# Reordering one stretch of a fused attention and MLP kernel: kv a little later, two transposes together, one weight chunk earlier, one output later

## The chip, the cores and the metric

The kernel runs on one core of one Trainium2 chip. The metric is the device time of one execution in microseconds (us). In the profile, PE is TensorE, PEld its weight loads, DVE is VectorE, ACT ScalarE, POOL GpSimd, SP SyncE.

## The reference, cut to what matters

```python
def _attn_ref(q, k, v, phi):          # batch 8, heads 8, seq 576, head_dim 64, phi has 32 memory slots
    a = softmax(phi, axis=slots)
    k_m = einsum('bhsm,bhsd->bhmd', a, k)        # pooled k
    v_m = einsum('bhsm,bhsd->bhmd', a, v)        # pooled v
    attn = softmax(scale * q @ k_m^T)
    return attn @ v_m

def _moe_ref(x, g_ln, w_ch1, w_ch2):  # x: 8 x 576 x 512
    xn = layernorm(x) * g_ln
    return x + relu(xn @ w_ch1) @ w_ch2          # 512 -> 2048 -> 512
```

(Shortened; in the original the softmaxes and the norm are written out.) The kernel folds the pooled v into the first MLP weight: it makes W1b = pooled v times w_ch1 for each batch and then h = relu(W1b applied to the attention), so that the attention's output is never multiplied by w_ch1 itself.

Of the kernel before, what the change touches and what calls it, by code (L numbers as in the profile page):

```python
# [16 lines left out]
def kernel(  # L17
# [38 lines left out]
    def big(shape, dtype, name):  # L56
        return psum.tile(shape, dtype, name=name, tag="big", bufs=3)

    def one(shape, dtype, name):
        return psum.tile(shape, dtype, name=name, tag="one", bufs=2)  # L60
# [35 lines left out]
    def load(b):  # L96
        loaded[b] = (phis[b] if b > 2 else load_phi(b, nc.gpsimd), load_kv(b), load_q(b))
# [137 lines left out]
    def a_kv(b):  # L235
        ps = big([P, 2, 512], FP32, "kv_ps")
        kv_mm(b, ps, slice(0, 2))
        if b < 2:
            kv_sum(b, ps)
            rs_out(b, ps)  # L240
        k_out(b, ps, True)
        v_out(b, ps[:, :, D:2 * D])

    def a_tr(b, k_part=True, v_part=True):
        s = st8[b]
        t_ps = big([P, 3, P], BF16, "kvT_ps")
        if k_part:
            kvT = att.tile([P, 3, P], BF16, name="kvT")
            s["kvT"] = kvT
            for g in range(2):  # L250
                nc.tensor.transpose(t_ps[:, g, :], s["k2"][:, g].rearrange("p a d -> p (a d)"), ident)
        kvT = s["kvT"]
        if v_part:
            nc.tensor.transpose(t_ps[:, 2, :], s["v2"].rearrange("p a d -> p (a d)"), ident)
        if k_part:
            nc.vector.tensor_copy(out=kvT[:, 0:2, :], in_=t_ps[:, 0:2, :])
        if v_part:
            nc.vector.tensor_tensor(out=kvT[:, 2, :].rearrange("p (j m) -> p j m", m=M),  # L258
                                    in0=t_ps[:, 2, :].rearrange("p (j m) -> p j m", m=M),
                                    in1=g_bf.unsqueeze(2).to_broadcast([P, 4, M]), op=ALU.mult)  # L260
            rsum = att.tile([P, 2], FP32, name="rsum")
            nc.vector.tensor_reduce(out=rsum, in_=s["v2"], axis=mybir.AxisListType.X, op=ALU.add)
            s["rsum"] = rsum
# [9 lines left out]
    def a_vb(b):  # L273
        s = st8[b]
        vb = att.tile([P, 2, 4, D], BF16, name="vb", bufs=3)
        for g in range(2):
            vsl = s["v2"][:, g, :].unsqueeze(1).to_broadcast([P, 4, D])
            nc.vector.tensor_tensor(out=vb[:, g], in0=vsl, in1=vmask, op=ALU.mult)
        s["vb"] = vb

    def a_qT(b, i):
        s = st8[b]
        if b > 1:

            if i == 0:
                s["qT"] = att.tile([P, 4, NP, P], BF16, name="qT")
                nc.sync.dma_start_transpose(out=s["qT"].rearrange("p j n x -> p (j n) x"),
                                            in_=s["q"].rearrange("p j n x -> p (j n x)"))
            return
        if i == 0:  # L290
            s["qT"] = att.tile([P, 4, NP, P], BF16, name="qT")
        q_ps = big([P, 2, 1024], BF16, "qT_ps")
        for u in range(2):
            for n in range(NP):
                nc.tensor.transpose(q_ps[:, u, P * n:P * (n + 1)], s["q"][:, 2 * i + u, n, :], ident)
        dst = s["qT"][:, 2 * i:2 * i + 2].rearrange("p a n x -> p a (n x)")
        if i == 0 or b == 1:
            nc.scalar.activation(out=dst, in_=q_ps[:, :, 0:NP * P], func=AF.Copy)
        else:
            nc.vector.tensor_copy(out=dst, in_=q_ps[:, :, 0:NP * P])  # L300

    def a_sc(b):
        s = st8[b]
        kvT, qT = s["kvT"], s["qT"]
        E_ = att.tile([P, 2, 2 * HP], BF16, name="E_sb", bufs=1)
        for g in range(2):
            sc = big([P, 2, 512], FP32, "sc_ps")
            for j in range(4):
                for r in range(2):
                    nc.tensor.matmul(  # L310
                        sc[32 * j:32 * (j + 1), r, 0:HP],
                        kvT[64 * r:64 * (r + 1), g, 32 * j:32 * (j + 1)],
                        qT[64 * r:64 * (r + 1), j, :, TS * g:TS * (g + 1)],
                        start=True, stop=True, tile_position=(64 * r, 32 * j))
            nc.scalar.activation(out=E_[:, g].rearrange("p (a x) -> p a x", a=2),  # L315
                                 in_=sc[:, :, 0:HP], func=AF.Exp, scale=s["rs"][:, g:g + 1])
        s["E"] = E_

    def a_den(b, finish=True):
        s = st8[b]  # L320
        Eh = att.tile([P, 2, S], BF16, name="Eh", bufs=3)
        rd = att.tile([P, 2, 2, HS], FP32, name="rden", bufs=1)
        for g in range(2):
            den = big([P, 2, 512], FP32, "den_ps")
            for half in range(2):
                o = HS * half
                nc.tensor.matmul(den[:, half, 0:HS], blk, s["E"][:, g, o:o + HS],  # L327
                                 start=True, stop=True)
            nc.scalar.activation(out=rd[:, g], in_=den[:, :, 0:HS], func=AF.Ln)  # L329
        s["Eh"], s["rd"] = Eh, rd  # L330
        if finish:
            a_den2(b)

    def a_den2(b):
        s = st8[b]
        Eh, rd = s["Eh"], s["rd"]
        for g in range(2):
            nc.scalar.activation(out=rd[:, g], in_=rd[:, g], func=AF.Exp, scale=-1.0)  # L338
            nc.vector.scalar_tensor_tensor(  # L339
                out=Eh[:, g, :], in0=s["E"][:, g, 0:S],  # L340
                scalar=s["rs"][:, g:g + 1], in1=rd[:, g].rearrange("p a x -> p (a x)"),
                op0=ALU.mult, op1=ALU.mult)

    def a_w1b(b, n):
        s = st8[b]
        if n == 0:
            s["w1b"] = att.tile([P, 2, F], BF16, name="w1b", bufs=1)
        ps = big([P, 2, 512], FP32, "w1b_ps")
        fs = slice(512 * n, 512 * (n + 1))
        for j in range(4):  # L350
            for g in range(2):
                r = 64 * g
                nc.tensor.matmul(  # L353
                    ps[32 * j:32 * (j + 1), g, :], s["kvT"][r:r + 64, 2, 32 * j:32 * (j + 1)],
                    w1r[r:r + 64, j, fs], start=True, stop=True, tile_position=(r, 32 * j))
        for g in range(2):
            nc.vector.scalar_tensor_tensor(  # L357
                out=s["w1b"][:, g, fs], in0=m_sb[:, fs], scalar=s["rsum"][:, g:g + 1],
                in1=ps[:, g, :], op0=ALU.mult, op1=ALU.add)
# [72 lines left out]
    def mm2(pr, t, j0, j1, ps=None, finish=True):  # L432
        rT = pair[pr]
        if j0 == 0:
            chs[(pr, t)] = one([P, C], FP32, "ch_ps") if ps is None else ps
        ch_ps = chs[(pr, t)]
        for j in range(j0, j1):
            nc.tensor.matmul(ch_ps, rT[:, j, P * t:P * (t + 1)], w2b[:, j, :],  # L438
                             start=(j == 0), stop=(j == JC - 1))
        if j1 == JC and finish:  # L440
            mm2_out(pr, t)
# [17 lines left out]
    def mm2_out(pr, t):  # L459
        ch_ps = chs[(pr, t)]  # L460
        x, rstd = xs[(pr, t)]
        nc.vector.scalar_tensor_tensor(out=x, in0=ch_ps, scalar=rstd, in1=x,  # L462
                                       op0=ALU.mult, op1=ALU.add)
        for u in range(2):
            lo = P * t + TS * u
            dst = out[2 * pr + lo // S].rearrange("(p c) x -> c p x", c=NS)
            nc.sync.dma_start(out=dst[CO[lo % S // TS]], in_=x[TS * u:TS * (u + 1), :])
# [61 lines left out]
    a_exp(1)  # L529
    mm2(0, 0, 4, 16)  # L530
    mm2(0, 1, 4, 16)
    mm2(0, 2, 0, 4)
    a_kv(1)
    mm2(0, 2, 4, 8)
    a_tr(1)
    a_qT(1, 0)
    a_w1b(1, 0)
    mm2(0, 2, 8, 12)
    a_qT(1, 1)
    a_w1b(1, 1)  # L540
    mm2(0, 2, 12, 16)
    a_sc(1)
    mm2(0, 3, 0, 4)
    a_den(1)
    a_w1b(1, 2)
    mm2(0, 3, 4, 8)
    a_w1b(1, 3)
    a_vb(1)
    mm2(0, 3, 8, 16)
    load(2)  # L550

    for b in range(1, B):
# [69 lines left out]
```

## The kernel before: the parts that the change touches

There are three PSUM buffers of two banks each, which nearly all intermediate results share, and two of one bank for the output sums (PSUM is the memory that the matmuls write into):

```python
def big(shape, dtype, name):
    return psum.tile(shape, dtype, name=name, tag="big", bufs=3)
def one(shape, dtype, name):
    return psum.tile(shape, dtype, name=name, tag="one", bufs=2)
```

The steps of one batch's attention, cut to what each engine does:

```python
def a_kv(b):      # PE: pooled k and v -> kv_ps; ACT, DVE: read them out
def a_tr(b):      # PE: transposes of pooled k and v -> kvT_ps; DVE: read out
def a_qT(b, i):   # PE: ten transposes of half i of q -> qT_ps; ACT: read out (batch 1)
def a_sc(b):      # PE: scores -> sc_ps (two halves g); ACT: E_sb = exp(scores)
def a_den(b, finish=True):   # PE: sums of E_sb -> den_ps; ACT: ln, then exp(-ln); DVE: Eh = E_sb / sum
    ...
    if finish:
        a_den2(b)
def a_w1b(b, n):  # PE: chunk n of four of W1b -> w1b_ps; DVE: two evictions into w1b
    ...
    for g in range(2):
        nc.vector.scalar_tensor_tensor(
            out=s["w1b"][:, g, fs], in0=m_sb[:, fs], scalar=s["rsum"][:, g:g + 1],
            in1=ps[:, g, :], op0=ALU.mult, op1=ALU.add)
def mm1(b, j0, j1):   # PE: 4 matmuls per j -> h_ps; ACT or DVE: Relu into rT
def mm2(pr, t, j0, j1, ps=None, finish=True):   # PE: j1-j0 matmuls of output tile t -> ch_ps
    ...
    if j1 == JC and finish:
        mm2_out(pr, t)    # DVE: x = x + rstd * ch_ps; SP: two stores
```

In the traces here each engine's instructions come in the order of the program. From batch 2 on, a batch's attention is threaded into the ch_ps matmuls of the pair before by a general loop. Batch 1's is threaded by hand into those of batch 0, and this is the list that the change reorders:

```python
mm2(0, 1, 4, 16)
mm2(0, 2, 0, 4)
a_kv(1)
mm2(0, 2, 4, 8)
a_tr(1)
a_qT(1, 0)
a_w1b(1, 0)
mm2(0, 2, 8, 12)
a_qT(1, 1)
a_w1b(1, 1)
mm2(0, 2, 12, 16)
a_sc(1)
mm2(0, 3, 0, 4)
a_den(1)
a_w1b(1, 2)
mm2(0, 3, 4, 8)
a_w1b(1, 3)
a_vb(1)
mm2(0, 3, 8, 16)
load(2)
...
mm1(1, 0, JC)
```

The softmax here doesn't subtract the row's maximum and nothing guards it: scores larger than these inputs give would overflow.

## Time and profile before

| what | value |
|---|---|
| time, median of 3 runs | 257.77 us (257.45 to 258.12) |
| span of the profiled execution | 256.2 us |
| PE busy | 241.3 us, 94% |
| kv_ps of batch 1 starts | 42.86 us |
| first h_ps of batch 1 starts | 54.79 us |
| the 64 h_ps of batch 1 end | 58.97 + 5.15 = 64.12 us |

A row of a timeline has start and duration in us, engine, line, operation, out<-in, shape and count; in brackets stands how long the engine was idle before it and what ended that. I use one more number throughout: **from kv_ps to the end of h_ps**, here 64.12 - 42.86 = 21.26 us. It is meant to leave out when v landed.

### The profile page before, as it was taken

Reading aid. Unit: us, or ns where it says so; the run is one execution under the profiler, and the core shown is the slowest. Engines: PE = TensorE matmul, PEld = TensorE weight load, DVE = VectorE, ACT = ScalarE, POOL = GpSimd, SP = SyncE. Lnnn points to the kernel's source line nnn. Section 1 sums busy time; section 2 is a strip of 40 time slices with the busy share of each in tenths; the row PEclk is TensorE's granted clock in tenths of the full one; section 3 lists DMA queues with packets and bytes.
Section 4 is the critical chain, followed back from the end, with each engine's and each line's share of the span. In section 5 each row is a group of like instructions: output and inputs, shape, how many; then the busy total and the mean of one; then the engine's idle time right before and its main releaser. Section 6 shows DMA issues by size and latency. Waiting matters only on the chain.

```text
span 256.2 us, 5777 instructions
## 1 busy us (share of the span) xinstructions
PE 241.3 (94%) x2421; PEld 131.6 (51%) x2453; DVE 154.8 (60%) x306; ACT 129.0 (50%) x219; POOL 51.9 (20%) x87
## 2 busy tenths in 40 slices
PE   7968998999989999999999999999999999999994
PEld 2534554447534574457544664457444764466453
DVE  3236772675495954695486746694577648683431
ACT  3155662666545483547544582558253762565210
POOL 8642330000720007100630009000800022000000
PEclk9999999999999999999999999999999999999999
DMA  7999999999399383997399492969398441130133
GB/s 152 186 206 206 207 254 231 267 185 129 111 166 194 84 162 96 183 199 142 97 177 193 93 214 38 210 159 157 107 197 179 103 84 44 45 73 9 44 82 82
DMA packets 41922, 36.82 MB, mean 144 GB/s; under 512 B 17444, under 2 KB 37160, under 8 KB 41896
## 3 DMA queue, kind: packets, MB, share of 16 engines
q0 software_dynamic: 17248, 19.53, 44.9%
q1 hardware_dynamic: 24488, 16.79, 28.6%
q8 instruction: 19, 0.31, 0.5%
q10 hardware_dynamic: 160, 0.13, 0.2%
q14 instruction: 7, 0.06, 0.1%
HBM read 41.42 MB, written 9.44 MB: 199 GB/s over the span
## 4 chain that ended last, share of the span: by engine, by line
PE 81%; DMA 6%; DVE 4%; ACT 3%; POOL 2%; issue 2%; POOLq 0%
PE ch_ps L438 44%; PE h_ps L374 24%; DMA w1r<-in_moe_w_ch_dram 6%; PE w1b_ps L353 3%; PE o_ps L404 2%; PE kv_ps L205 2%; DVE w1b L357 2%; PE last_ps L450 1%; PE den_ps L327 1%; POOL kv_bf L84 1%; PE sc_ps L310 1%; DVE bst L416 1%; ACT rT L380 1%; POOL q_bf L92 1%; DVE Eh L339 1%
## 5 line engine op out<-in xcount | busy, mean ns | idle before, releaser
L438 PE MATMUL ch_ps<-w2b,rT 128*128 128x512 bf16 x530 | 126.0, 380 | 2.1 <-issue 1.1
L438 PEld LDWEIGHTS <-rT 128*128 128x128 bf16 x560 | 51.1, 98 | 62.6 <-issue 7.4
L374 PE MATMUL h_ps<-Eh,w1b 128*128 128x288 bf16 x512 | 67.4, 285 | 1.2 <-ACT rT L380 0.7
L380 ACT ACTIVATE rT<-h_ps 128x576 bf16<-128x576 f32 x88 | 52.6, 649 | 22.7 <-PE h_ps L374 22.5
L374 PEld LDWEIGHTS <-w1b 128*128 128x128 bf16 x512 | 49.5, 97 | 18.6 <-issue 2.9
L357 DVE SCALAR_TENSOR_TENSOR w1b<-m_sb,rsum,w1b_ps 128x512 bf16<-128x512 f32 x64 | 43.7, 742 | 3.2 <-ACT m_sb L169 2.4
L382 DVE TENSOR_SCALAR rT<-h_ps 128x576 bf16<-128x576 f32 x40 | 30.3, 757 | 24.1 <-PE h_ps L374 24.1
L410 ACT ACTIVATE x_sb<-o_ps 128x1024 f32<-128x1024 f32 (+1 forms) x20 | 18.6, 937 | 37.8 <-PE o_ps L404 36.5
L462 DVE SCALAR_TENSOR_TENSOR x_sb<-ch_ps,rstd,x_sb 128x512 f32<-128x512 f32 x35 | 26.1, 746 | 15.0 <-PE ch_ps L438 14.3
L189 POOL TENSOR_TENSOR es<-e_sb 128x512 f32<-128x512 bf16 x6 | 6.9, 1152 | 139.1 <-ACT e_sb L182 139.1
L416 DVE BATCH_NORM_STATS2 bst<-x_sb 128x6 f32<-128x512 f32 x36 | 24.4, 678 | 8.1 <-ACT x_sb L410 8.1
L339 DVE SCALAR_TENSOR_TENSOR Eh<-E_sb,rs,rden 128x576 bf16<-128x576 bf16 x16 | 12.4, 816 | 15.9 <-ACT rden L338 15.9
L315 ACT ACTIVATE E_sb<-sc_ps,rs 128x640 bf16<-128x640 f32 x16 | 11.9, 790 | 12.1 <-PE sc_ps L310 12.1
L424 ACT ACTIVATE rstd<-mv,eps_sb 128x2 f32<-128x2 f32 (+1 forms) x20 | 5.9, 296 | 20.3 <-DVE mv L417 20.3
L353 PE MATMUL w1b_ps<-w1r,kvT 64*32 64x512 bf16 x256 | 10.8, 383 | 0.9 <-DVE kvT L258 0.4
L174 PE MATMUL w_ps<-fill 128*128 128x512 f32 x14 | 9.7, 815 | 1.6 <-DVE fill L119 1.6
L227 DVE CAST v<-kv_ps 128x128 bf16<-128x128 f32 x8 | 2.3, 292 | 14.6 <-ACT k L220 13.7
L329 ACT ACTIVATE rden<-den_ps 128x576 f32<-128x576 f32 x16 | 9.6, 644 | 2.1 <-PE den_ps L327 2.1
L182 ACT ACTIVATE e_sb<-phi_st 128x1152 bf16<-128x1152 f32 x8 | 9.2, 1152 | 2.6 <-DMA phi_st<-in_phi_dram 2.6
L338 ACT ACTIVATE rden<-rden 128x576 f32<-128x576 f32 x16 | 10.0, 680 | 0.0
L205 PEld LDWEIGHTS <-e_sb 64*32 64x32 bf16 x648 | 6.3, 90 | 6.3 <-ACT e_sb L182 3.0
L205 PE MATMUL kv_ps<-kv_bf,e_sb 64*32 64x128 bf16 (+1 forms) x648 | 7.5, 214 | 1.9 <-issue 0.8
(69 smaller groups left out, 143.6 us busy)
## 6 DMA issues: line engine op xcount, KB each, us to landing
out_dram<-x_sb SPq DMA_DIRECT2D x70, 128.0 KB, 2.4
kv_bf<-in_k_dram POOLq DMA_DIRECT2D x7, 576.0 KB, 6.4
kv_bf<-in_v_dram POOLq DMA_DIRECT2D x7, 576.0 KB, 9.6
phi_st<-in_phi_dram SPq DMA_DIRECT2D x6, 576.0 KB, 4.5
q_bf<-in_q_dram POOLq DMA_DIRECT2D x6, 576.0 KB, 11.9
w1r<-in_moe_w_ch_dram POOLq DMA_DIRECT2D x4, 512.0 KB, 14.3
w2b<-in_moe_w_ch_dram POOLq DMA_DIRECT2D x4, 512.0 KB, 18.7
q_bf<-in_q_dram POOLq DMA_DIRECT2D x4, 288.0 KB, 12.5
```

What stands on the lines that cost most here:

```text
L205: nc.tensor.matmul(ps[32 * j:32 * (j + 1), g, 0:D * (sl.stop - sl.start)], e[r:r + TS, c, j, :], kv[r:r + TS, j, sl, D * c:D * (c + 1)], s ...
L315: nc.scalar.activation(out=E_[:, g].rearrange("p (a x) -> p a x", a=2), in_=sc[:, :, 0:HP], func=AF.Exp, scale=s["rs"][:, g:g + 1])
L339: nc.vector.scalar_tensor_tensor(out=Eh[:, g, :], in0=s["E"][:, g, 0:S], scalar=s["rs"][:, g:g + 1], in1=rd[:, g].rearrange("p a x -> p (a ...
L353: nc.tensor.matmul(ps[32 * j:32 * (j + 1), g, :], s["kvT"][r:r + 64, 2, 32 * j:32 * (j + 1)], w1r[r:r + 64, j, fs], start=True, stop=True, ...
L357: nc.vector.scalar_tensor_tensor(out=s["w1b"][:, g, fs], in0=m_sb[:, fs], scalar=s["rsum"][:, g:g + 1], in1=ps[:, g, :], op0=ALU.mult, op1 ...
L374: nc.tensor.matmul(h_ps[:, half, 0:HS], s["w1b"][:, g, P * j:P * (j + 1)], s["Eh"][:, g, HS * half:HS * (half + 1)], start=(g == 0), stop= ...
L380: nc.scalar.activation(out=dst, in_=h_ps[:, :, 0:HS], func=AF.Relu)
L382: nc.vector.tensor_scalar(out=dst, in0=h_ps[:, :, 0:HS], scalar1=0.0, scalar2=None, op0=ALU.max)
L410: nc.scalar.activation(out=x[:, 0:n].rearrange("p i (u y) -> p i u y", u=2), in_=o_ps.rearrange("p u (i y) -> p i u y", i=2)[:, 0:n], func ...
L416: nc.vector.bn_stats(out=stt, in_=x[:, i, :])
L438: nc.tensor.matmul(ch_ps, rT[:, j, P * t:P * (t + 1)], w2b[:, j, :], start=(j == 0), stop=(j == JC - 1))
L462: nc.vector.scalar_tensor_tensor(out=x, in0=ch_ps, scalar=rstd, in1=x, op0=ALU.mult, op1=ALU.add)
```

## The change

Its intent is to fill PE's pauses in this stretch: kv is asked for later, when v has landed; the two q transposes stand together, so that ScalarE can read them out one behind the other; the third W1b chunk goes ahead of the denominators; the output of tile 3 goes behind the last W1b. No instruction is added or taken away.

```diff
     mm2(0, 1, 4, 16)
-    mm2(0, 2, 0, 4)
+    mm2(0, 2, 0, 8)
     a_kv(1)
-    mm2(0, 2, 4, 8)
+    mm2(0, 2, 8, 12)
     a_tr(1)
     a_qT(1, 0)
+    a_qT(1, 1)
     a_w1b(1, 0)
-    mm2(0, 2, 8, 12)
-    a_qT(1, 1)
+    mm2(0, 2, 12, 16)
     a_w1b(1, 1)
-    mm2(0, 2, 12, 16)
     a_sc(1)
     mm2(0, 3, 0, 4)
+    a_w1b(1, 2)
     a_den(1)
-    a_w1b(1, 2)
-    mm2(0, 3, 4, 8)
+    mm2(0, 3, 4, 12)
     a_w1b(1, 3)
+    mm2(0, 3, 12, 16, finish=False)
     a_vb(1)
-    mm2(0, 3, 8, 16)
+    mm2_out(0, 3)
     load(2)
```

## The prediction

> **What bounds the kernel now.** I read the page first, then the chain of work in order of time, then the timelines of the engines in the one stretch that the change touches.
>
> ```profile
> PE 241.3 (94%) x2421; PEld 131.6 (51%) x2453; DVE 154.8 (60%) x306; ACT 129.0 (50%) x219; POOL 51.9 (20%) x87
> ...
> PE 81%; DMA 6%; DVE 4%; ACT 3%; POOL 2%; issue 2%; POOLq 0%
> ```
>
> TensorE (PE) is busy 94% of the 256.2 us span and is 81% of the chain that ended last, so the kernel is as long as PE's work plus PE's pauses. The change removes and adds no instruction and reorders only the stretch in which batch 1's attention is threaded into the second matmul (ch_ps) of batch 0. Of all that can happen, only PE's pauses in that stretch count. The stretch is from the end of the ch_ps matmuls of tile 1 (42 us) to the end of batch 1's h_ps group (64.2 us). In the chain in order of time its parts that are not PE's work are:
>
> ```profile
> 42.06 0.80 issue
> 42.86 0.93 PE kv_ps L205 x72
> ...
> 49.54 1.48 ACT E_sb L315 x2
> 51.02 1.14 ACT rden L329 x2
> 52.16 0.58 ACT rden L338
> ...
> 52.76 1.55 DVE Eh L339 x2
> 54.31 1.33 DVE w1b L357 x2
> ```
>
> The reader should see a pause of 0.8 us ahead of kv_ps that the profile cannot name ("issue"), and then a chain through ScalarE and VectorE from the scores (sc_ps) to h_ps. The unnamed pause gets its name from where the transfers were issued and how long each took to land; the first block is GpSimd's timeline, the second the list of transfers (size, us from issue to landing) for each of these two issues alone:
>
> ```profile
> 23.25 0.74 POOL L84 DMA_DIRECT2D kv_bf<-in_v_dram  x1 [1.80 <-DMA w1r<-in_moe_w_ch_dram]
> ...
> 28.38 0.71 POOL L92 DMA_DIRECT2D q_bf<-in_q_dram  x1 [1.88 <-DMA w2b<-in_moe_w_ch_dram]
> ```
> ```profile
> kv_bf<-in_v_dram POOLq DMA_DIRECT2D x1, 576.0 KB, 19.5
> ...
> q_bf<-in_q_dram POOLq DMA_DIRECT2D x1, 288.0 KB, 18.3
> ```
>
> So batch 1's v lands at 23.25 + 19.5 = 42.75, and kv_ps starts at 42.86: the pause is a wait for v. The second half of q lands at 28.38 + 18.3 = 46.7 (the first, issued at 25.80 and 19.1 us under way, at 44.9). PE's own rows show when they are used, and two further pauses:
>
> ```profile
> 47.13 0.72 PE L295 MATMUL qT_ps<-ident,q_bf 128*128 128x128 bf16 x10
> ...
> 51.07 0.41 PE L327 MATMUL den_ps<-E_sb,blk 128*128 128x288 bf16 x2 [0.22 <-ACT E_sb L315]
> ...
> 55.69 1.15 PE L374 MATMUL h_ps<-Eh,w1b 128*128 128x288 bf16 x8 [0.24 <-DVE w1b L357]
> 57.09 1.63 PE L374 MATMUL h_ps<-Eh,w1b 128*128 128x288 bf16 x12 [0.25 <-ACT rT L380]
> ```
>
> The first q transpose runs at 45.17, the second at 47.13, only 0.4 us after its data landed. The h_ps group pauses three times (55.69, 57.09 and 58.97). A printed pause runs from the modelled end of the last matmul, so I count from starts instead: the 64 h_ps matmuls of batch 2 take 7.96 us in the chain (124 ns each), batch 1's take from 54.79 to 64.17, 9.38, so 1.2 to 1.4 us is lost there. By starts the pause at kv_ps is 0.9 us, at den_ps 0.4, at the v transpose (45.10) 0.3, at the first w1b_ps (45.91) 0.2, at sc_ps 0.1. **All pauses of the stretch come to about 3.1 us, 1.2% of 257.77.** That is the most that this reordering could take away.
>
> **What the Trainium skill says.** "Perfetto Trace Analysis", section "Optimization Strategy": find the gaps on the engine that should be full and the semaphore that ends each. That is the method here. "PSUM — Partial Sum Buffer", section "Engine vs sequencer instructions": matmuls start and complete in program order, and the queues of ScalarE and VectorE are strict FIFOs. The trace agrees: ch_ps matmuls that were ready stood behind kv_ps in the 0.8 us pause, and the W1b evictions stand behind Eh from 52.76 on. "DMA: Bandwidth & Descriptors", section "Two DMAs through the same engine are not ordered": data has landed once the full semaphore increment is in. The trace agrees: kv_ps starts 0.1 us after v's landing. "TensorE: Matmul & The Clock Gate", section "Back-to-back issue gap": an isolated matmul of N columns issues in N/2.4 + 2.5 ns, 216 ns for N = 512. The trace has 4.10 us for 19 ch_ps, 216 ns each, so four of them, the unit in which the change moves things, are 0.86 us.
>
> **The change part by part.**
> (1) kv four matmuls later. PE reaches kv at 41.9 + 0.86 = 42.8 in place of 41.9; v lands at 42.75. kv still starts at about 42.86, with the wait filled by useful matmuls: **-0.85 us**. Four ch_ps still stand between kv and the transposes of k and v, so the 0.3 us pause there stays.
> (2) Both q transposes at once. The first starts at 45.17 as now and issues its 10 at 56 ns in 0.56 us, to 45.73. The second then stands at the head of PE's queue at 45.75, but its half of q lands at 46.68 (28.38 + 18.3). No store or load ahead of it is moved, so it will land at the same time. In the kernel before the w1b_ps of chunk 0 and four ch_ps (0.34 + 0.87 us) covered this. New wait: 46.72 - 45.75, **+0.95 us**. It swallows the 0.2 us pause before the first w1b_ps (-0.2), as kvT is ready at 45.86.
> (3) From there to the scores the work is the same (w1b_ps twice at 0.35, four ch_ps 0.87, a few tenths of switching): transposes to 47.28, w1b_ps 47.37, ch_ps 47.7 to 48.6, w1b_ps 48.67, sc_ps at 49.03. It needs ScalarE's eviction of the second transpose: 47.5 + 1.24 = 48.7, done. **sc_ps at 49.03 against 49.09: nothing gained, -0.1 at most.** E_sb follows at 49.5 to 50.95.
> (4) Third W1b chunk ahead of the denominators. PE reaches it at 50.46; with E_sb's first half read from its bank pair at 50.3 there is room and no wait. Its 0.34 us fills PE while E_sb's second half is made, which takes most of the 0.4 us pause at den_ps. But the third of the three two-bank PSUM buffers holds chunk 1, whose eviction now stands behind tile 2's output on VectorE (moved ahead of it): chunk 0 47.85 to 49.26, output to 49.95, chunk 1 to 51.3. So one den_ps starts at 51.0 and the other at 51.35, about half a microsecond later than now (50.44, 51.07). Ln, Ln, Exp, Exp on ScalarE (0.65, 0.65, 0.67, 0.67, overlapping a little) then give Eh at 54.1 and 54.85, now 53.58 and 54.31. **Pause at den: 0.45 us, against 0.4.**
> (5) Eight ch_ps, the fourth chunk and four ch_ps (1.73 + 0.43 + 0.87) bring PE to h_ps at 54.65, now 54.79, and Eh is just ready. Only one chunk's eviction (1.4 us) is left behind Eh in place of the two that the chain shows now (54.23 to 56.95). The pause at the second h_ps (0.4 us) goes. The third h_ps needs a buffer: from the fourth chunk (56.2) or from the first h_ps (0.65 us of Relu, 56.0), so 0.4 us of waiting comes back there; the later two pauses, 0.4 each, shrink to about 0.5 in all. **1.2 becomes 0.9 us, -0.3.**
> (6) Tile 3's output behind the last W1b: on VectorE it stood there already, -0.0.
>
> Sum: -0.85 + 0.95 - 0.2 - 0.1 + 0.05 - 0.3 = **-0.45 us, so 257.3 us**. All after 64.2 us follows PE rigidly and shifts as a block: batch 2's loads were issued by 38 us and its q had landed before 58.
>
> **The rivals.**
> *The wait for q does not bite* (q's second half lands a microsecond earlier than in this trace, or the stores of tiles 0 and 1 disturb it less). Then (2) costs nothing and scores, denominators and h_ps all come 0.9 us earlier: 256.4. [...]Against: its landing is 18.3 us after issue, in line with the 19.5 and 19.1 ahead of it, and nothing earlier is changed.
> *Buffers tie chunk 2 to chunk 1.* If the third chunk is given the buffer that chunk 1 leaves at 51.3 instead of the scores', PE stands still 0.9 us at 50.46 and Eh comes 0.5 us later than in (4): h_ps at 55.2, some of it won back in fewer pauses: 257.9. For it: the order of buffers is not visible in the profile. Against: E_sb frees a pair a microsecond sooner.
> *All pauses go.* If the reordering did what it is for at every point, it would win about 3 us: 254.7. Against: the v transpose, Eh and the first Relus are chains of ScalarE and VectorE that no part of the change shortens.
>
> **Range and chances.** The three runs before spread by 0.67 us, the rivals by 256.4 to 257.9. I take 256.3 to 258.2 for 8 in 10. Two per cent is 5.2 us: faster by that is more than all the pauses there are (0.01), slower would need a wait of 5 us where no transfer or eviction is that late (0.02). Same: 0.97.
>
> **What would show it.** Right: kv_ps still at 42.8 to 42.9, now without a pause; a pause of about 0.9 us between the two groups of ten q transposes, ended by the q transfer; sc_ps within 0.2 us of 49.1; den_ps at 51.0 to 51.4; a single W1b pair behind Eh on VectorE. Wrong: the second q transposes at 45.8, or h_ps starting outside 54.3 to 55.3, or the end of h_ps moved by over 1 us against 64.17. A change after 64.2 us beyond this shift would also refute it.

## The result, and the profile after

The changed kernel took 256.51 us (median of 4 runs, 256.24 to 257.01), the kernel before beside it 257.89 us. The ratio is 0.9951, with a 95% interval of 0.9928 to 0.9973: 0.5% faster, some 1.3 us. A ratio here is the mean time of one kernel's fast runs over that of the other's fast runs of the same rounds, so it is not quite the ratio of the medians. By the 2% measure the two are the same.

The chain of work of the changed kernel in order of time, in the stretch (start, length, what):

```profile
27.89 18.13 DMA q_bf<-in_q_dram
46.02 0.05 issue
46.07 0.73 PE qT_ps L295 x10
...
50.31 0.74 PE den_ps L327 x4
...
54.08 0.50 PE h_ps L374 x4
54.59 0.02 issue
54.61 0.66 ACT rT L380
55.27 0.04 issue
55.31 7.14 PE h_ps L374 x56
```

Three things differ from before. The chain now comes in through the transfer of q. From the second q transpose to h_ps it is all PE's own work, where before it left PE at the scores (49.54) and came back at h_ps (55.69) by way of ScalarE and VectorE. And h_ps has one pause for a Relu of ScalarE, after which 56 matmuls run through. PE's timeline shows the new wait and how the scores and h_ps lie:

```profile
46.07 0.73 PE L295 MATMUL qT_ps<-ident,q_bf 128*128 128x128 bf16 x10 [0.65 <-DMA q_bf<-in_q_dram]
...
48.26 0.74 PE L310 MATMUL sc_ps<-qT,kvT 64*32 64x320 bf16 x16
```

VectorE's timeline tells what became of the W1b evictions. Before, four of them stood behind Eh:

```profile
54.23 2.72 DVE L357 SCALAR_TENSOR_TENSOR w1b<-m_sb,rsum,w1b_ps 128x512 bf16<-128x512 f32 x4
```

After, those of chunk 2 follow chunk 1's ahead of Eh, in time in which VectorE had stood idle before (2.43 us ahead of Eh, by the same view), and two stand behind it:

```profile
49.20 2.71 DVE L357 SCALAR_TENSOR_TENSOR w1b<-m_sb,rsum,w1b_ps 128x512 bf16<-128x512 f32 x4
52.49 1.54 DVE L339 SCALAR_TENSOR_TENSOR Eh<-E_sb,rs,rden 128x576 bf16<-128x576 bf16 x2 [0.58 <-ACT rden L338]
53.96 1.40 DVE L357 SCALAR_TENSOR_TENSOR w1b<-m_sb,rsum,w1b_ps 128x512 bf16<-128x512 f32 x2
```

The spans of the two profiles differ by 1.7 us (256.2 and 254.5), but 0.5 us of this lies ahead of anything that was changed: in the second execution v was issued at 22.76 in place of 23.25, and landed 19.5 us later in both. From kv_ps to the end of h_ps the changed kernel takes 55.31 + 7.14 - 42.37 = 20.08 us, 1.18 less than before. Behind the end of h_ps both have 192.1 us left, as have all 12 experiments (192.05 to 192.08). The effect is therefore made between these two points and passed on unchanged. PE's own clock agrees: reckoned back from the last ch_ps ahead of kv_ps, at 0.216 us each, PE began tile 2, where the two programs part, at 41.03 and 40.54 us; v landed 1.74 us after that in both, and h_ps ended 23.08 and 21.92 us after that.

### The profile page after: what moved, and what is told of

The parts are those of the page before. It is cut to its first block, busy times and chain, and to the rows that moved or that the text cites. A ratio compares the mean times of both kernels' runs of the same rounds, so it can differ in the third digit from the quotient of the medians.

```text
span 254.5 us, 5778 instructions
## 1 busy us (share of the span) xinstructions
PE 241.0 (95%) x2422; PEld 131.6 (52%) x2453; DVE 155.0 (61%) x306; ACT 129.1 (51%) x219; POOL 51.8 (20%) x87
## 4 chain that ended last, share of the span: by engine, by line
PE 76%; DMA 17%; DVE 3%; issue 2%; ACT 1%; POOL 1%; POOLq 0%
PE ch_ps L438 42%; PE h_ps L374 22%; DMA q_bf<-in_q_dram 7%; DMA w2b<-in_moe_w_ch_dram 6%; DMA kv_bf<-in_k_dram 3%; PE w1b_ps L353 3%; PE o_ps L404 2%; PE kv_ps L205 2%; PE den_ps L327 2%; PE last_ps L450 1%; PE sc_ps L310 1%; DVE bst L416 1%; POOL q_bf L92 1%; DVE w1b L357 1%; ACT x_sb L410 0%
## 5 line engine op out<-in xcount | busy, mean ns | idle before, releaser
L92 POOL DMA_DIRECT2D q_bf<-in_q_dram x10 | 7.6, 757 | 4.6 <-DMA w2b<-in_moe_w_ch_dram 1.9
```

## The experiments

Twelve runs were made, of nine new kernels, two of these again and the changed kernel again, four to a call, each with five rounds; all gave correct results. As nothing behind h_ps differs, only the stretch is told. "kv to h_ps" is from the start of kv_ps to the start of h_ps, "h_ps" is the length of the group of 64, both in the profiled execution.

| run | ratio to before (95%) | kv to h_ps | h_ps | sum | pauses in h_ps |
|---|---|---|---|---|---|
| before | | 11.94 | 9.32 | 21.26 | 0.40, 0.41, 0.41 |
| the change | 0.9951 (0.9928 to 0.9973) | 11.55 | 8.53 | 20.08 | 0.41 |
| e1_kv_only | 0.9994 (0.9977 to 1.0012) | 11.92 | 9.32 | 21.24 | 0.40, 0.41, 0.41 |
| e2_w1b2_only | 0.9977 (0.9958 to 0.9996) | 11.42 | 8.60 | 20.01 | 0.41 |
| e3_w1b2_back | 1.0002 (0.9984 to 1.0020) | 12.22 | 9.37 | 21.59 | 0.44, 0.41, 0.41 |
| e4_q_apart | 0.9970 (0.9945 to 0.9994) | 11.55 | 8.60 | 20.14 | 0.41 |
| e5_evict_first | 0.9964 (0.9943 to 0.9984) | 11.93 | 8.48 | 20.41 | 0.35 |
| e6_matmul_first | 0.9998 (0.9975 to 1.0020) | 11.42 | 9.87 | 21.28 | 0.90, 0.41, 0.41 |
| e7_tuned | 0.9943 (0.9918 to 0.9968) | 11.47 | 8.60 | 20.06 | 0.41 |
| e8_tuned_fill | 0.9938 (0.9916 to 0.9960) | 10.31 | 9.03 | 19.34 | 0.48 |
| after_again | 0.9971 (0.9944 to 0.9998) | 12.18 | 8.53 | 20.71 | 0.41 |
| e2_again | 0.9957 (0.9933 to 0.9981) | 11.42 | 8.59 | 20.01 | 0.41 |
| e9_out_in_place | 0.9957 (0.9931 to 0.9983) | 10.96 | 8.58 | 19.54 | 0.41 |
| e8_again | 0.9954 (0.9930 to 0.9979) | 10.95 | 9.04 | 19.99 | 0.49 |

(Pauses are counted from starts: the distance of two h_ps starts less 0.123 us; only those over 0.2 us. In e8 there is another distance of 0.43 us where two ch_ps stand between h_ps; it is work and no pause. The times of single runs of a kernel spread by 1 us and more, so that the columns from the trace separate what the ratios only group.)

One caution about the sum. In e1, e9 and e8_tuned_fill v had landed 0.57, 0.56 and 0.21 us before kv_ps began; in all other profiles 0.09 us before. In these three it was PE that came late, after the ch_ps put ahead of kv. From v's landing to the end of h_ps they take 21.81, 20.09 and 19.55 us, against 21.35 before, 20.18 and 20.80 in the two profiles of the change and 20.10 in both of e2. So e9's lead in the table is only the place where the count begins.

**Theory A**: the gain is made in h_ps by the third W1b chunk, and filling the wait for v only hands the wait on. **Rival B**: the filled wait for v is the gain, as the prediction's step 1 books it, and the chunk adds a little.

### e1_kv_only: the later kv alone

```diff
-mm2(0, 2, 0, 4)
+mm2(0, 2, 0, 8)
 a_kv(1)
-mm2(0, 2, 4, 8)
+mm2(0, 2, 8, 12)
 a_tr(1)
 a_qT(1, 0)
 a_w1b(1, 0)
-mm2(0, 2, 8, 12)
+mm2(0, 2, 12, 16)
 a_qT(1, 1)
 a_w1b(1, 1)
-mm2(0, 2, 12, 16)
 a_sc(1)
```

> One part alone: the kernel before with batch 1's kv moved four ch_ps matmuls later (they are taken from ahead of the scores; the rest as before). Theory A (the gain is made in the h_ps group by the third W1b chunk; filling the wait for v only hands the wait on to the q transposes or the scores, which hang on the landing of q and on ScalarE's 1.24 us eviction): kv_ps starts at the same time without its pause, but a pause of about 1 us appears ahead of sc_ps, and the time stays within 0.2 us of before. Rival B (filling the wait for v is worth what it covers, as step 1 of the prediction books it): 0.8 us faster than before.

Measured: ratio 0.9994, and 21.24 us in the stretch against 21.26. In PE's timeline the wait has moved to the scores, whose last three quarters stand until ScalarE has read out the second q transpose:

```profile
48.12 0.31 PE L310 MATMUL sc_ps<-qT,kvT 64*32 64x320 bf16 x4
49.28 0.45 PE L310 MATMUL sc_ps<-qT,kvT 64*32 64x320 bf16 x12 [0.86 <-ACT qT L298]
```

By starts this pause is 1.11 us, about the 0.86 us of ch_ps that were taken from there and the pause of 0.1 us that stood there before. In this profile v came early, so less of a wait was filled than before's 0.96 us, and from v's landing the stretch is 0.46 us longer than before. The ratio of all six runs allows a gain of 0.6 us at most, where rival B asked for 0.8. Theory A holds here and rival B falls.

### e2_w1b2_only: the third W1b chunk alone

```diff
 mm2(0, 3, 0, 4)
-a_den(1)
 a_w1b(1, 2)
+a_den(1)
 mm2(0, 3, 4, 8)
```

> One part alone: the kernel before with the third W1b chunk put ahead of the denominators and nothing else. Theory A: two of the three pauses of the h_ps group go (0.8 us), den_ps loses its pause of 0.4 us to the chunk, while Eh comes some 0.3 us later, which PE does not feel: 0.8 to 1.2 us faster than before. Rival B: 0.3 to 0.4 us faster.

Measured: ratio 0.9977, 20.01 us in the stretch: 1.25 less than before, a little more than the whole change made. The ratio's 0.6 us was under the 0.8 to 1.2 that Theory A asked for, so this kernel was run again (below). In the chain of work h_ps now has one pause, for a Relu, and 56 matmuls in one piece:

```profile
54.75 0.57 PE h_ps L374 x4
55.32 0.02 issue
55.35 0.66 ACT rT L380
56.00 0.04 issue
56.05 7.14 PE h_ps L374 x56
```

### e3_w1b2_back: the change without the chunk's move

```diff
 mm2(0, 3, 0, 4)
-a_w1b(1, 2)
 a_den(1)
+a_w1b(1, 2)
 mm2(0, 3, 4, 12)
```

> One part undone: the changed kernel with the third W1b chunk behind the denominators again. Theory A: the scores stay 0.3 to 0.4 us earlier than before, but the h_ps group has its three pauses of 0.4 us back: 0.2 to 0.5 us faster than before, so 0.8 us slower than the changed kernel. Rival B: 0.8 to 0.9 us faster than before, 0.4 slower than the changed kernel.

Measured: ratio 1.0002. All three pauses in h_ps are back. The small gain that Theory A left to the other parts did not show: in this execution the second half of q landed 19.4 us after its issue and the joined transposes waited 1.35 us for it, so that h_ps began later than before. Beside e2 and e4, run on the same chip in the same rounds, it shows that the gain of the change hangs on this one line; by the ratios alone the intervals of the three overlap.

### e4_q_apart: the change with the q transposes apart

```diff
 a_qT(1, 0)
-a_qT(1, 1)
 a_w1b(1, 0)
 mm2(0, 2, 12, 16)
+a_qT(1, 1)
 a_w1b(1, 1)
```

> One part undone: the changed kernel with the second q transpose behind the first W1b chunk and four ch_ps matmuls again. Theory A: no pause for q any more, but the transposed q leaves ScalarE 0.5 us later, so that the scores start at 49.1 to 49.2 (in before's time) in place of 48.8 with a pause of about 1 us ahead of them: 0.7 to 1.0 us faster than before, 0.2 to 0.5 slower than the changed kernel. Rival B (the wait for q in the changed kernel costs what it shows): 0.6 us faster than the changed kernel.

Measured: ratio 0.9970, 20.14 us. The wait for q is gone and a pause of 1.11 us ahead of most of the scores has come, as in e1; the end is within 0.1 us of the change's. So a wait of 0.8 us that stands plainly in the profile of the changed kernel cost nothing against this order, which has a wait of its own in its place. Theory A had expected 0.2 to 0.5 us worse, so it was too pessimistic here; rival B's 0.6 us better did not come.

### e5_evict_first and e6_matmul_first: the chunk's move taken in two

e5 leaves the chunk's matmuls behind the denominators' and moves only its evictions ahead of Eh:

```diff
-a_den(1)
+a_den(1, finish=False)
 a_w1b(1, 2)
+a_den2(1)
 mm2(0, 3, 4, 8)
```

> The move of the third W1b chunk taken apart, on the kernel before. Here its matmuls stay behind those of the denominators, and only its two evictions on VectorE go ahead of the two Eh. If the gain has two parts (the buffer comes free earlier for h_ps, 0.8 us; the matmuls fill the pause at den_ps, 0.4 us), this has the first alone: one pause of 0.4 us in the h_ps group in place of three, the pause of 0.4 us at den_ps still there, Eh 0.5 us later; 0.6 to 0.8 us faster than before. If only the filled pause at den_ps counts: no gain, or up to 0.3 us slower for the later Eh.

e6 does the reverse (`a_w1b` got a parameter that holds back its two evictions and returns them):

```diff
-a_den(1)
-a_w1b(1, 2)
+w1b2 = a_w1b(1, 2, evict=False)
+a_den(1)
+w1b2()
 mm2(0, 3, 4, 8)
```

> The other half: the third chunk's matmuls go ahead of the denominators', its evictions stay behind the two Eh. If the gain has two parts, this has the second alone: h_ps starts up to 0.4 us earlier, but with its three pauses of 0.4 us each; 0.2 to 0.4 us faster than before. If the buffer alone counts: no gain, and since the chunk's buffer is now held for 4 us by an eviction that waits, perhaps 0.5 us slower.

Measured: e5 0.9964 and 20.41 us, 0.85 less than before: h_ps starts when it did and has one pause. VectorE's timeline shows the third chunk's evictions ahead of Eh and only the fourth's behind it:

```profile
51.85 1.41 DVE L357 SCALAR_TENSOR_TENSOR w1b<-m_sb,rsum,w1b_ps 128x512 bf16<-128x512 f32 x2 [1.55 <-PE w1b_ps L353]
53.17 1.54 DVE L339 SCALAR_TENSOR_TENSOR Eh<-E_sb,rs,rden 128x576 bf16<-128x576 bf16 x2
54.63 1.40 DVE L357 SCALAR_TENSOR_TENSOR w1b<-m_sb,rsum,w1b_ps 128x512 bf16<-128x512 f32 x2
```

e6 0.9998 and 21.28 us: h_ps starts 0.52 us earlier, somewhat more than the 0.4 expected, and loses all of it again. No gain was the forecast of its second branch; the gain of 0.2 to 0.4 us of the first did not come. The pauses of its h_ps in PE's timeline (the last row is cut where the view ends):

```profile
53.96 0.72 PE L378 MATMUL h_ps<-Eh,w1b 128*128 128x288 bf16 x4
55.42 1.14 PE L378 MATMUL h_ps<-Eh,w1b 128*128 128x288 bf16 x8 [0.74 <-ACT rT L384]
56.80 1.63 PE L378 MATMUL h_ps<-Eh,w1b 128*128 128x288 bf16 x12 [0.25 <-ACT rT L384]
58.68 1.51 PE L378 MATMUL h_ps<-Eh,w1b 128*128 128x288 bf16 x11 [0.25 <-ACT rT L384]
```

The second h_ps here waits for the Relu of the first. The built programs say why, by the banks that they give to each buffer; the pauses in the traces fall where these make one wait. These are the first banks (2, 4 or 6) of the three buffers as h_ps takes them in turn, with those of the third and fourth chunk:

```
before   w1b 4, w1b 2, h: 6 4 6 4 2 6 2 4 6 2 4 6 ...
change   w1b 6, w1b 4, h: 2 6 2 4 6 2 4 6 2 4 6 2 ...
e6       w1b 2, w1b 6, h: 4 4 2 4 6 2 6 4 2 6 4 2 ...
e5       w1b 4, w1b 2, h: 6 4 2 6 4 2 6 4 2 6 4 2 ...
```

While chunks wait for their evictions behind Eh, their buffers are missing for h_ps. In e6 two are held, and one is left. In the kernel before, the second h_ps waits for the third chunk's evictions, the third has to take the buffer of the first, the fourth that of the second, and the seventh that of the fifth. In the change only one chunk is held when h_ps starts, and after the third h_ps the buffers go round by three. A reordering of the program thus changes both the queue on VectorE and the order in which the buffers are handed out, and no run separates these two. The two halves of the move don't simply add: the eviction ahead of Eh is worth 0.85 us alone; the matmuls ahead of the denominators are worth 0.5 us at the start of h_ps, which lasts only when the evictions come early too.

### after_again, e2_again and e9_out_in_place: side by side

after_again is the changed kernel and e2_again that of e2, both unchanged. e9 undoes the last part of the change:

```diff
 a_den(1)
-mm2(0, 3, 4, 12)
+mm2(0, 3, 4, 8)
 a_w1b(1, 3)
-mm2(0, 3, 12, 16, finish=False)
 a_vb(1)
-mm2_out(0, 3)
+mm2(0, 3, 8, 16)
```

> The changed kernel once more, as the measure for the three beside it on the same chip. Both theories: 1.0 to 1.5 us faster than before.

> The kernel before with the third W1b chunk ahead of the denominators and nothing else, once more, beside the changed kernel on the same chip. Theory A (this one move makes the whole gain): within 0.3 us of the changed kernel, and the stretch from tile 1's output to the end of h_ps 1.0 to 1.3 us shorter than before. Rival B (the later kv and the joined q transposes add to it): 0.5 us or more slower than the changed kernel.

> One part undone: the changed kernel with the last W1b chunk behind eight of tile 3's ch_ps matmuls instead of twelve, and tile 3's output not held back. VectorE meets these in the same order, and its evictions of that chunk wait for Eh anyway: within 0.2 us of the changed kernel. If the place of the last chunk mattered, the pause in h_ps would change by some tenths.

Measured: the changed kernel 0.9971, somewhat under the 1.0 to 1.5 us expected (0.75 us); e2_again 0.9957; e9 0.9957, 0.36 us ahead of the changed kernel where 0.2 was allowed, within the noise. The one-line kernel is not behind the whole change, and its stretch came out at 20.01 us again. In this execution of the changed kernel, q landed late:

```profile
47.84 0.73 PE L295 MATMUL qT_ps<-ident,q_bf 128*128 128x128 bf16 x10 [1.42 <-DMA q_bf<-in_q_dram]
```

Counted from the start of the second q transpose to the end of h_ps, both profiles of the change take 16.4 us, and so does e9, so tile 3's output and the place of the last chunk do nothing. e9's shorter sum in the table comes from where it begins: v had landed early, PE came to kv_ps 0.56 us after that, and so q had nearly landed when it was asked for (a pause of 0.22 us by starts).

### e7_tuned, e8_tuned_fill and e8_again: a version meant to beat both

```diff
 a_qT(1, 0)
-a_qT(1, 1)
 a_w1b(1, 0)
-mm2(0, 2, 12, 16)
+a_qT(1, 1)
+mm2(0, 2, 12, 16, finish=False)
 a_w1b(1, 1)
+mm2_out(0, 2)
 a_sc(1)
```

This puts 0.34 us of W1b work into the wait for q and tile 2's output behind the second chunk's evictions. e8 and e8_again also take the last two ch_ps of tile 3 from ahead of h_ps and put them between its second and third j.

> A version meant to beat the changed kernel: as that, with the first W1b chunk between the two q transposes (0.34 us of work in the wait for q) and tile 2's output behind the second chunk's eviction, so that the second den_ps does not wait for it. If after the third chunk's move PE's own pauses bind: 0.3 to 0.5 us faster than the changed kernel, 1.5 to 1.8 faster than before. If the chain from the scores through ScalarE to Eh binds: within 0.2 us of the changed kernel.

> As the version before, with the last two ch_ps matmuls of tile 3 held back to stand between the second and the third h_ps, where the changed kernel pauses 0.4 us for a buffer. If PE's pauses bind: a further 0.3 to 0.4 us faster, about 2 us faster than the kernel before. If Eh binds, h_ps begins with a new pause of up to 0.4 us and nothing is gained over the version before.

> The tuned version with two ch_ps held back, once more beside the changed kernel: in the first look q landed 0.8 us sooner than in the version without them, which may have made its lead. If the lead is its own: 0.5 us or more faster than the changed kernel. If it was q's landing: within 0.3 us of it.

Measured: 0.9943, 0.9938 and 0.9954. From the second q transpose to the end of h_ps they take 15.88, 15.92 and 15.91 us, 0.5 less than the changed kernel's 16.4 and as much as e2's (15.87), where the first W1b chunk stands ahead of this transpose too. In e7 q landed 0.5 us later after kv_ps than in the first profile of the change (4.13 against 3.65 us) and the sum is the same (20.06 and 20.08). So the tuned version would gain about 0.5 us on the change where q is late in both; this is an estimate from these traces, and the times do not show it. Holding back two ch_ps added nothing, as expected for the case that Eh binds: h_ps started earlier and then stood for Eh (PE's timeline of e8_tuned_fill):

```profile
53.36 0.41 PE L374 MATMUL h_ps<-Eh,w1b 128*128 128x288 bf16 x2
54.09 0.90 PE L374 MATMUL h_ps<-Eh,w1b 128*128 128x288 bf16 x6 [0.32 <-DVE Eh L339]
```

In the ratios e8_again (0.9954) does not stand clear of the changed kernel beside it (0.9971) nor of e2_again (0.9957). A version that surely beats the one-line change was not found.

## Why the prediction was right or wrong

It was right in its range (256.3 to 258.2), and wrong in its size: it said 0.45 us, the first look shows about 1.3, the second 0.75, and the stretch 1.18. That the range held is in part luck: the median of 256.51 lies near its lower end, two of the four runs (256.29 and 256.24) fall just below it, and the range reached so low for a rival that did not come true. One of its own signs of being wrong came true: the end of h_ps moved by over 1 us, by 1.18 on the clock used below. Of its signs of being right, two failed: sc_ps came 0.35 us before 49.1, and the first den_ps started at 50.73 where 51.0 to 51.4 was given. The wait for q and the single W1b pair behind Eh came as told. To compare clocks, 0.49 us is added here to the times of the changed kernel, so that kv_ps starts at 42.86 in both.

1. **kv later.** As predicted: kv_ps starts when v has landed, and its pause by starts went from 0.96 to 0.10 us. What the prediction did not draw from this is that the part alone is worth nothing: e1 shows a wait of the same kind again at the scores. Its -0.85 and the +0.95 for q are not two terms but one wait handed on, and as both are in the sum they did no harm to it. (One small reading was off: the pause at the v transpose, given as 0.3 us, is 0.17 by starts.)
2. **The wait for q.** It came, ended by q's transfer: 0.81 us by starts, 0.95 predicted; q took 18.1 us from issue to landing, 18.3 before. e4 shows that without this wait, and with one of 1.11 us at the scores in its place, the end is the same.
3. **Scores.** Predicted at 49.03, measured at 48.75. Of these 0.28 us, q's landing makes about 0.15. E_sb ended at 50.62 (predicted 50.95).
4. **Denominators.** The second den_ps waited for chunk 1's eviction as predicted, but by 0.15 us only, where 0.45 was booked for both, and the chunk's work filled the rest. h_ps started at 54.41 where 54.65 was predicted: 0.38 earlier than before in place of 0.14.
5. **The pauses in h_ps.** This is the term that was mis-sized most, and the step that failed. The pause at the second h_ps went and one of 0.41 us at the third came, both as predicted. But "the later two pauses, 0.4 each, shrink to about 0.5 in all" was wrong: they went altogether, as the buffers go round by three from the fourth h_ps on. The group went from 9.32 to 8.53, so -0.79 in place of -0.3.
6. **Tile 3's output.** Nothing, as predicted, and e9 agrees.

The sum closes: 0.24 us in the start of h_ps and 0.49 in its pauses, added to 0.45, make 1.18.

Of the rivals, "the wait for q does not bite" (256.4) comes near the time, but not for its reason: the wait stood in the trace, and in after_again it was nearly twice as long. "Buffers tie chunk 2 to chunk 1" did not happen: the compiled program gave the third chunk the bank pair of the scores (6).

How much the joined transposes lose on average, against e2's order, stays open: it depends on when q lands, which moved by a microsecond between executions. In the two profiles of the change the sum is 20.08 and 20.71 against e2's 20.01. Not all of the 0.7 us in the second is the order's fault: q landed 4.27 us after kv_ps began, and e2 asks for it at 4.14, so e2 would have waited for some 0.2 us too (an estimate from these traces).

## What to carry to other kernels

A wait that is filled at one place is no gain until the next thing that stands on the same chain is shown to move; the other parts of this change gained nothing that shows, one line gained 1.2 us in the stretch. When a matmul group pauses for buffers, look on the evicting engine for evictions that queue behind something late, and put those that are ready ahead of it, together with their matmuls. Separate what a change does from when the data landed: here a stretch of the trace told apart what five rounds of times left within half a per cent. Check in each trace that the stretch begins on the landing and not on the engine's own arrival; in three of the fourteen profiles here it did not.

## What the Trainium skill lacked or had wrong

- "TensorE: Matmul & The Clock Gate", section "Back-to-back issue gap", gives about 131 ns per matmul of 512 columns as what a real stream of weight loads and matmuls sustains, and says that N/2.4 + 2.5 over-counts there. In this kernel 19 ch_ps matmuls, each with its own weight load, took 4.10 us, 216 ns each, and the 64 h_ps of 288 columns of batch 2 took 7.96 us, 124 ns each: the formula called isolated (216 and 122.5) is what fits here.
- "Perfetto Trace Analysis", section "Optimization Strategy", says that consistent bubbles can mean too little SBUF or PSUM for the next tile. The three pauses of 0.40 to 0.41 us in h_ps were such bubbles, but went down to one with the same three buffers, by the order of the evictions on VectorE and the order of the buffers that follows from it (e5: 0.85 us). The page does not name this cause.
- None of the pages that I read tells how far a transfer's landing scatters between executions of one program: v of batch 1 landed 19.5 us after its issue in one profile of the changed kernel and 20.1 in the other, the second half of q 18.1 and 19.4.
